# Moving rows between partitions in batch 1 of an attention kernel: DMA transfers in place of VectorE copies

## The chip, the cores and the metric

The kernel runs on one core of a Trainium2 chip. The metric is the device time of one execution in microseconds (us). TensorE is called PE here, VectorE DVE, ScalarE ACT, GpSimd POOL, and SyncE SP; SP computes nothing in this kernel, it issues the DMA transfers.

## What is computed

Three layers run one after the other: an attention over hash buckets, a mixing layer (a Fourier transform over both axes, a normalisation, a feed-forward network) and a gated convolution. Only the first is touched by the change:

```python
def _attn_ref(q, k, v, proj):                 # q, k, v: 2 batches x 8 heads x 768 rows x 64
    scale = 1.0 / np.sqrt(D)
    q_bits = (np.einsum('bhsd,dk->bhsk', q, proj) > 0).astype(np.int64)   # proj: 64 x 6
    k_bits = (np.einsum('bhsd,dk->bhsk', k, proj) > 0).astype(np.int64)
    powers = 2 ** np.arange(n_bits)
    q_bucket = np.sum(q_bits * powers, axis=-1)
    k_bucket = np.sum(k_bits * powers, axis=-1)
    mask = q_bucket[:, :, :, None] == k_bucket[:, :, None, :]
    scores = scale * np.matmul(q, k.transpose(0, 1, 3, 2))
    scores = np.where(mask, scores, -1000000000.0)
    ...                                       # softmax over the last axis
    return np.matmul(attn, v).astype(np.float32)
```

The attention's output x (2 x 768 x 512) goes through `_moe_ref` (u = x + real part of the transform of x, then u + relu(norm(u) W1) W2) and `_moe2_ref` (sigmoid of a causal convolution, times x W, times W').

## The kernel before

The heads of a batch are taken two at a time: four pairs g = 0 to 3 in each of batches 0 and 1. For a pair, `prep(g)` makes the operands of the score matmuls, and then three units of 256 query rows follow (`pair` and `unit_out`), each with two heads and two blocks of 128 rows.

`prep` splits q and k into a high and a low fp16 part (`st`), transposes both with one DMA transpose each (line 248) into the tile `tb` (128 partitions: high and low part, each 64 deep), and fills a second tile `ta`, whose rows are contracted in a second matmul of the same scores. Three of `ta`'s pieces are rows of `tb` or `ta` that must stand on other partitions, and the function `move` brings them there:

- line 251, q: `ta[0:64, 0]` from `tb[64:128, 0]`, 64 partitions x 1536 fp16 values
- line 252, k: `ta[0:64, 1]` from `tb[0:64, 1]`, the same size
- line 266, the sign features of the hash: `ta[64:96, 1]` from `ta[96:128, 0]`, 32 partitions x 1536 values. DVE writes these signs at line 265 from the products `bt` of line 260 (PE).

A score matmul (line 326) reads `ta` and then `tb`. DVE reads the scores out of PSUM into `e` with their maximum (line 338), ACT takes the exponential (line 343) and its fp16 part (line 112), POOL the rest (line 120), and a DMA transpose (line 355, `at<-a`) turns the result, so that PE can multiply it with v (line 364, `pv`).

`QJ` is a pair of strings, one for each batch; each letter says who performs one of the three moves: `v` is DVE, `s` a DMA issued by SP.

A scheduler that simulates the program places the instructions: what stands in the code in one order is merged, for each engine, into one fixed list. So batch 1's pair 0 is prepared while batch 0's last units run, the mixing layer of batch 0 (lines 480 to 682) is woven into batch 1's pair 0, and the feed-forward network of batch 0 (lines 712 and 729) into batch 1's pairs 1 to 3. Each engine takes its list in order: an instruction that waits holds up all that stand behind it. This holds for SP too. Its list contains the loads of q, k and v (lines 211 and 213), the loads of weights into a ring of two slots (line 433, `ring`), which DVE unpacks with three instructions (lines 419 to 421), and all DMA transposes. A DMA that reads what another DMA wrote is issued once SP has seen the first one land.

Of the kernel before, what the change touches and what calls it, by code (L numbers as in the profile page):

```python
# [46 lines left out]
LEFT = 512  # L47
WB = 512
QW = {None: "s", "w2": "s"}
QJ = ('vvv', 'vvv')  # L50
TPE = {(0, g, i, 1): 'a' for g in range(4) for i in (1,)}
PPE = {(0, 1): 'a'}
HI = {}
# [24 lines left out]
def attention_fft_mix_gated_kernel(  # L78
# [121 lines left out]
    def attention(b, P, after=None):  # L200
# [15 lines left out]
        def move(o, i, eng):  # L216
            if eng in "vga":
                copy_of(o, i, 1.0, eng)
            else:
                nc.sync.dma_start(out=o, in_=i)  # L220
# [9 lines left out]
        def prep(g):  # L230
# [12 lines left out]
            for y in range(2):  # L243
# [3 lines left out]
                else:  # L247
                    marks[b, "prep", g] = nc.sync.dma_start_transpose(
                        out=tb[:, y].rearrange("p h (c t) -> p (h c) t", t=128), in_=it
                    ).ins  # L250
            move(ta[0:64, 0], tb[64:128, 0], QJ[b][0])
            move(ta[0:64, 1], tb[0:64, 1], QJ[b][1])
            for n in range(2):
# [9 lines left out]
                for hh in range(2):  # L263
                    o = slice(64 * hh, 64 * hh + 64)
                    nc.vector.tensor_scalar(ta[64:128, 0, hh, r], bt[o, :], lim[o, 0:1], lim[o, 1:2], ALU.is_gt, ALU.mult)
            move(ta[64:96, 1], ta[96:128, 0], QJ[b][2])
            values(g, lv)
            tq[g] = ta, tb

        def values(g, lv):  # L270
            vt = P.vt.tile([128, 2, C, 2, D], FP16, tag="vt", name="vt")
            v2 = vt.rearrange("p h c x d -> p (h c) x d")
            with after_mark([marks["first", PF]] if not b and g == 0 else []):
                split(v2[:, :, 0, :], v2[:, :, 1, :], lv, VS, 'av' if not b and g < 1 else VH[b])
            va[g] = vt
# [828 lines left out]
```

## Time and profile before

| what | us |
|---|---|
| median of three runs | 684.14 |
| lowest and highest of them | 683.41 and 687.34 |
| the profiled execution's own time | 682.82 |
| its span, first to last instruction | 681.0 |
| PE busy in the span | 578.8 (85%) |
| DVE busy | 521.9 (77%) |
| ACT busy | 367.0 (54%) |
| POOL busy | 283.4 (42%) |

The profile is that of one execution; the span leaves out 1.8 us that lie around it. Where times of instructions are given they count from the start of the span. Busy times of the whole span hide that the stages have different limits, so the stretch from 132 to 381 us, where batch 1's attention runs, has to be read by itself.

### The profile page before, as it was taken

What the parts mean: (1) busy time and instruction counts of PE and PEld (TensorE: products, weight loads), DVE (VectorE), ACT (ScalarE), POOL (GpSimd) and SP (SyncE); (2) the same over time, 40 slices, a digit from 0 to 9 for tenths busy, and PEclk for the clock granted to TensorE, in tenths of its full rate; (3) what the DMA queues carried; (4) which work ended last, traced back from release to release, by engine and by line L of the source; (5) the groups of instructions that cost most, each with busy time, mean ns of one, the idle gap of its engine ahead of it and who ended that gap; (6) DMA issues with size and microseconds to landing.
All of it is one profiled execution on the core that took longest, in us unless ns stands there. A gap on an engine that the chain in (4) does not pass through costs nothing.

```text
span 681.0 us, 13258 instructions
## 1 busy us (share of the span) xinstructions
PE 578.8 (85%) x5078; PEld 443.7 (65%) x5078; DVE 521.9 (77%) x1007; ACT 367.0 (54%) x752; POOL 283.4 (42%) x312
## 2 busy tenths in 40 slices
PE   6787767866537789986999999988999999999997
PEld 3454535544324657665677788877677788888864
DVE  6978797799999898998865369996999256282682
ACT  4997979996764337875888426311334202111242
POOL 3868668875864415767656301260232100000000
PEclk8787779787866689999999999998799999999999
DMA  8989999989776354689785764000000000000001
GB/s 300 236 139 234 210 234 217 225 133 179 149 153 139 110 124 109 148 155 198 139 145 102 135 183 151 6 1 1 1 32 32 32 1 2 2 1 1 1 32 63
DMA packets 177888, 75.84 MB, mean 111 GB/s; under 512 B 162464, under 2 KB 168224, under 8 KB 177824
## 3 DMA queue, kind: packets, MB, share of 16 engines
q1 hardware_dynamic: 177248, 74.88, 50.6%
q8 instruction: 40, 0.66, 0.4%
q14 instruction: 24, 0.20, 0.1%
q10 hardware_dynamic: 576, 0.10, 0.1%
HBM read 32.50 MB, written 3.15 MB: 52 GB/s over the span
## 4 chain that ended last, share of the span: by engine, by line
PE 30%; DVE 13%; ACT 3%; issue 3%; POOL 1%; ACTq 0%; DVEq 0%; POOLq 0%
PE f L729 14%; PE f L712 8%; DVE gt L754 3%; PE op L873 2%; PE vp L848 1%; PE vp L770 1%; ACT a L112 1%; PE op L795 1%; DVE x L126 1%; DVE gt L117 1%; DVE h L694 1%; ACT e L343 1%; DVE cen L644 1%; PE mp L601 1%; DVE gt L821 1%
## 5 line engine op out<-in xcount | busy, mean ns | idle before, releaser
L120 POOL TENSOR_TENSOR a<-e,a 128x384 f16<-128x384 f32 x184 | 174.9, 976 | 93.0 <-ACT a L112 75.7
L712 PE MATMUL f<-un,w 128*128 128x256 f16 x1152 | 135.3, 274 | 3.2 <-DVE h L694 2.7
L729 PE MATMUL f<-h,w 128*128 128x256 f16 x1152 | 133.1, 274 | 0.9 <-DVE h L694 0.9
L712 PEld LDWEIGHTS <-w 128*128 128x128 f16 x1152 | 112.7, 98 | 22.0 <-issue 4.8
L729 PEld LDWEIGHTS <-w 128*128 128x128 f16 x1152 | 112.2, 98 | 17.8 <-issue 3.2
L338 DVE TENSOR_SCALAR_CACHE_REDUCE e<-sc 128x768 f32<-128x768 f32 x96 | 90.5, 949 | 16.1 <-POOL a L120 12.6
L364 PE MATMUL pv<-at,vt 128*64 128x256 f16 x864 | 75.3, 323 | 26.4 <-DMA at<-a 23.4
L343 ACT ACTIVATE e<-e,mx 128x768 f32<-128x768 f32 x96 | 89.1, 929 | 3.7
L364 PEld LDWEIGHTS <-vt 128*64 128x64 f16 x864 | 58.0, 130 | 44.7 <-issue 23.7
L112 ACT ACTIVATE a<-e 128x768 f16<-128x768 f32 x96 | 80.1, 839 | 1.0
L326 PE MATMUL sc<-ta 96*128 96x384 f16 x192 | 51.4, 352 | 29.8 <-DVE e L338 26.0
L694 DVE SCALAR_TENSOR_TENSOR h<-f,h 128x512 f16<-128x512 f32 x48 | 32.7, 686 | 32.7 <-ACT h L693 32.6
L326 PE MATMUL sc<-tb 128*128 128x384 f16 x192 | 51.9, 353 | 0.0
L693 ACT ACTIVATE h<-f 128x512 f16<-128x512 f32 x48 | 28.4, 591 | 43.1 <-PE f L712 42.9
L326 PEld LDWEIGHTS <-ta 96*128 96x128 f16 x192 | 17.0, 100 | 51.1 <-issue 44.6
L700 DVE SCALAR_TENSOR_TENSOR xb<-f,xb 128x256 f32<-128x256 f32 x24 | 13.7, 615 | 43.6 <-PE f L729 43.6
L120 POOL TENSOR_TENSOR w<-wt,w 128x256 f16<-128x256 f32 x40 | 30.1, 764 | 35.4 <-ACT w L112 35.2
L112 ACT ACTIVATE x<-xb 128x256 f16<-128x256 f32 x24 | 11.7, 535 | 54.0 <-DVE xb L700 53.5
L420 DVE SCALAR_TENSOR_TENSOR wt<-ring,wt 128x256 int32<-128x256 int32 (+1 forms) x60 | 37.0, 623 | 0.6
L821 DVE SCALAR_TENSOR_TENSOR gt<-xb,cw,gt 128x256 f32<-128x256 f32 x60 | 37.2, 680 | 0.0
L112 ACT ACTIVATE wt<-wt 128x256 f32<-128x256 f32 x40 | 16.2, 412 | 37.7 <-DVE wt L421 36.7
L421 DVE SCALAR_TENSOR_TENSOR wt<-ring,wt 128x256 int32<-128x256 int32 (+1 forms) x60 | 35.7, 602 | 0.5
(147 smaller groups left out, 930.6 us busy)
## 6 DMA issues: line engine op xcount, KB each, us to landing
ring<-in_moe_w_ch_dram SPq DMA_DIRECT2D x40, 256.0 KB, 3.1
ring<-in_moe_w_ch_dram SPq DMA_DIRECT2D x12, 512.0 KB, 5.0
lv<-in_v_dram SPq DMA_DIRECT2D x8, 384.0 KB, 4.5
out_dram<-ob SPq DMA_DIRECT2D x12, 256.0 KB, 2.0
lq<-in_q_dram SPq DMA_DIRECT2D x7, 384.0 KB, 3.9
lk<-in_k_dram SPq DMA_DIRECT2D x7, 384.0 KB, 4.6
ring<-in_moe_w_val_dram SPq DMA_DIRECT2D x4, 512.0 KB, 5.6
ring<-in_moe_w_out_dram SPq DMA_DIRECT2D x4, 512.0 KB, 3.9
```

The costliest lines, as they stand in the source:

```text
L112: return nc.scalar.activation(out=o, in_=i, func=ACTF.Copy, scale=s)
L120: return (nc.gpsimd if eng == "g" else nc.vector).tensor_tensor(out=o, in0=i0, in1=i1, op=op)
L326: nc.tensor.matmul(out=s[:, n, 0:384], lhsT=z[0:rows, 0, hh, r], rhs=z[0:rows, 1, hh, n * 384:n * 384 + 384], start=(x == 0), stop=(x == 1),)
L338: nc.vector.tensor_scalar(e.rearrange("p (a b) -> p a b", a=2), s, -(PEN * PEN) / 2, None, ALU.max, ALU.max, accum_out=m[:, 0:1]).ins
L343: marks["first", 2 + j] = nc.scalar.activation(out=e, in_=e, func=ACTF.Exp, bias=m[:, 1:2], scale=SC, accum_out=sums[:, hh, j:j + 1]).ins
L364: nc.tensor.matmul(out=p[64 * hh:64 * hh + 64, :], lhsT=va[g][:, hh, c, x, :], rhs=at[hh][:, :, y, c, :], start=(c == 0 and n == 0), stop= ...
L420: nc.vector.scalar_tensor_tensor(out=tmp, in0=hi, scalar=-0x40000000, in1=tmp, op0=ALU.bitwise_and, op1=ALU.bitwise_or)
L421: return nc.vector.scalar_tensor_tensor(out=dst, in0=lo, scalar=29, in1=tmp, op0=ALU.logical_shift_right, op1=ALU.bitwise_or)
L694: nc.vector.scalar_tensor_tensor(out=h[:, 1, f:f + 2, :], in0=p, scalar=0.0, in1=h[:, 0, f:f + 2, :], op0=ALU.max, op1=ALU.subtract)
L712: nc.tensor.matmul(out=p[:, o, :], lhsT=w1[:, i, kd, (f + o) * 128:(f + o) * 128 + 128], rhs=un[:, j, kd, :], start=(k == 0), stop=(k == 3 ...
L729: nc.tensor.matmul(out=p[:, o, :], lhsT=w2[:, i, f, (d + o) * 128:(d + o) * 128 + 128], rhs=h[:, j, f, :], start=(k == 0), stop=(k == 3 * ...
L821: nc.vector.scalar_tensor_tensor(out=o, in0=src, scalar=cw[:, d, j:j + 1].bitcast(FP32), in1=o, op0=ALU.mult, op1=ALU.add)
```

## The change

The second string of `QJ` becomes `sss`: in batch 1, all three moves of each of the four pairs are DMA transfers from SBUF to SBUF, issued by SP (line 220), where DVE copies (line 116) stood. Batch 0 keeps its copies.

```diff
--- before
+++ after
@@ -47,7 +47,7 @@
 LEFT = 512
 WB = 512
 QW = {None: "s", "w2": "s"}
-QJ = ('vvv', 'vvv')
+QJ = ('vvv', 'sss')
 TPE = {(0, g, i, 1): 'a' for g in range(4) for i in (1,)}
 PPE = {(0, 1): 'a'}
 HI = {}
```

Since the scheduler places every instruction, the lists of all engines differ from this point on. On SP, where batch 1's pair 0 is prepared (the transposes `tb<-st` are those of this pair, `at<-a` those of batch 0's last units):

```order
 L213 DMA lv<-in_v_dram 128x2x384
 L248 DMA_TRANSPOSE tb<-st 128x12x128 x2
+L220 DMA ta<-tb 64x1536
+L213 DMA lq<-in_q_dram 128x2x384
+L220 DMA ta<-tb 64x1536
+L213 DMA lk<-in_k_dram 128x2x384
+L355 DMA_TRANSPOSE at<-a 128x12x128 x3
+L220 DMA ta<-ta 32x1536
+L355 DMA_TRANSPOSE at<-a 128x12x128 x3
```

The two moves of q and k now stand between the transposes that they wait for and the `at<-a` transposes; the move of the signs stands among these.

On DVE, the same place (`e,mx<-sc` reads scores, `xb<-pv` scales a unit's output, `ta<-bt` makes the signs, `wt<-ring` unpacks weights):

```order
 L126 SCALAR_TENSOR_TENSOR vt<-lv,vt 128x12x64
-L116 COPY ta<-tb 64x1536
-L338 TENSOR_SCALAR e,mx<-sc 128x768
-L116 COPY ta<-tb 64x1536
-L338 TENSOR_SCALAR e,mx<-sc 128x768
+L338 TENSOR_SCALAR e,mx<-sc 128x768 x2
 L380 TENSOR_TENSOR xb_67<-pv,xb_67 128x256
 L265 TENSOR_SCALAR ta<-bt,lim 64x384 x2
 L371 RECIPROCAL r_1915<-r_1915 128x4
```

The two copies are gone and the rest closes up. Behind this piece the third copy is gone as well, and the mixing layer's instructions (lines 480 to 483, 126, 117) come earlier relative to the first scores of batch 1: on PE, twelve matmuls of line 503 now stand ahead of these scores.

On SP, at the last pair of batch 1, pair 3:

```order
 L248 DMA_TRANSPOSE tb<-st 128x12x128
-L355 DMA_TRANSPOSE at<-a 128x12x128 x24
+L433 DMA ring_2128<-in_moe_w_ch_dram 128x512
+L220 DMA ta<-tb 64x1536 x2
+L355 DMA_TRANSPOSE at<-a 128x12x128 x4
+L220 DMA ta<-ta 32x1536
+L355 DMA_TRANSPOSE at<-a 128x12x128 x20
```

Here too the moves of q and k stand ahead of all transposes that are left, and the signs' move behind four of them.

## Rows read from the trace of the kernel before

**Rows 1.** The page: busy time by engine, and the second feed-forward matmul's group.

```profile
PE 578.8 (85%) x5078; PEld 443.7 (65%) x5078; DVE 521.9 (77%) x1007; ACT 367.0 (54%) x752; POOL 283.4 (42%) x312
...
L729 PE MATMUL f<-h,w 128*128 128x256 f16 x1152 | 133.1, 274 | 0.9 <-DVE h L694 0.9
```

**Rows 2.** Busy time by stretch: bounds and length, then engines, PE clock, DMA share.

```profile
132.00:145.00 13.00, 9.05 (x103) 6.53 (x103) 12.71 (x23) 12.51 (x28) 7.76 (x8) 0.87 0.85 158
...
187.00:204.00 17.00, 5.92 (x49) 3.86 (x47) 16.94 (x31) 10.27 (x22) 11.46 (x12) 0.60 0.81 158
...
222.00:243.00 21.00, 14.47 (x122) 12.67 (x121) 18.44 (x41) 7.85 (x17) 7.53 (x10) 0.67 0.41 113
243.00:256.00 13.00, 12.49 (x87) 8.80 (x86) 11.20 (x25) 4.11 (x11) 1.97 (x3) 0.87 0.41 108
...
289.00:307.00 18.00, 15.29 (x160) 11.62 (x159) 17.63 (x35) 13.94 (x32) 12.28 (x15) 1.00 0.88 162
307.00:323.00 16.00, 11.14 (x106) 8.32 (x106) 13.27 (x24) 9.62 (x23) 11.55 (x13) 1.00 0.89 195
...
340.00:381.00 41.00, 40.66 (x390) 31.74 (x388) 22.48 (x45) 33.56 (x74) 22.32 (x26) 1.00 0.76 139
```

**Rows 3.** Groups of the copies, both batches: busy us, mean ns, idle before them.

```profile
L116 DVE COPY ta<-tb 64x1536 f16<-64x1536 f16 x14 | 9.8, 697 | 5.8 <-DMA tb<-st 5.6
L116 DVE COPY ta<-ta 32x1536 f16<-32x1536 f16 x7 | 5.2, 742 | 0.2
```

**Rows 4.** Timeline of DVE: start us, us, instruction, [idle before it].

```profile
132.54 0.55 DVE L116 COPY ta<-tb 64x1536 f16<-64x1536 f16 x1
...
133.99 0.85 DVE L116 COPY ta<-tb 64x1536 f16<-64x1536 f16 x1
...
144.82 0.56 DVE L116 COPY ta<-ta 32x1536 f16<-32x1536 f16 x1
...
146.86 0.96 DVE L338 TENSOR_SCALAR_CACHE_REDUCE e<-sc 128x768 f32<-128x768 f32 x1
...
147.75 1.22 DVE L126 SCALAR_TENSOR_TENSOR y<-yf,y 128x1024 f16<-128x1024 f32 x1
...
195.56 1.55 DVE L116 COPY ta<-tb 64x1536 f16<-64x1536 f16 x2
...
306.67 1.16 DVE L116 COPY ta<-ta 32x1536 f16<-32x1536 f16 x1
...
```

**Rows 5.** Timeline of SP: start us, us that issuing took, transfer.

```profile
127.45 4.47 SPq L248 DMA_TRANSPOSE tb<-st  x2
...
133.17 2.09 SPq L355 DMA_TRANSPOSE at<-a  x1
...
135.35 4.03 SPq L355 DMA_TRANSPOSE at<-a  x1
...
319.75 2.37 SPq L248 DMA_TRANSPOSE tb<-st  x1
...
322.23 1.46 SPq L355 DMA_TRANSPOSE at<-a  x1
```

**Rows 6.** DMA issues: transfer, count, KB each, median us from issue to landing.

```profile
out_dram<-ob SPq DMA_DIRECT2D x12, 256.0 KB, 2.0
...
at<-a SPq DMA_TRANSPOSE x88, 4.2
lq<-in_q_dram SPq DMA_DIRECT2D x2, 192.0 KB, 3.3
...
tb<-st SPq DMA_TRANSPOSE x12, 4.6
```

**Rows 7.** Timeline of PE, same columns as DVE's.

```profile
141.40 3.47 PE L364 MATMUL pv<-at,vt 128*64 128x256 f16 x36 [3.04 <-DMA at<-a]
...
145.43 0.48 PE L326 MATMUL sc<-ta 96*128 96x384 f16 x2
...
242.60 0.61 PE L712 MATMUL f<-un,w 128*128 128x256 f16 x4
...
307.88 0.48 PE L326 MATMUL sc<-ta 96*128 96x384 f16 x2 [1.17 <-DVE ta L116]
```

## The prediction

> **What bounds the kernel now.** I read the busy times of the whole span first [rows 1]: PE is busy for 85% of it and DVE for 77%, which looks like a kernel that PE alone limits. The table by stretch then says where that is true [rows 2]. From 340 us PE works for 40.66 of 41.00 us: there only PE's own work counts. Between 132 and 243 us it is DVE: 12.71 of 13.00 us, 16.94 of 17.00, 18.44 of 21.00, while PE is busy for about two thirds and its granted clock stands at 0.60 to 0.87, a mean between its two levels (1.2 and 2.4 GHz, 0.5 and 1.0). What DVE does there (batch 0's last units, batch 1's pair 0, the mixing layer) ends in the first feed-forward matmul at 242.60 [rows 7], and from then on PE has work for almost every gap. So a microsecond of DVE taken out before 242.60 is worth a microsecond, if nothing else becomes late; a microsecond taken out later is worth at most what PE idles: 0.51 us between 243 and 256, 2.71 between 289 and 307, 4.86 between 307 and 323 [rows 2]. The third thing to see is the DMA share: 0.85, 0.81, 0.88, 0.89 in the stretches where pairs are prepared [rows 2]. The twelve new transfers meet a loaded DMA.
>
> **What the change removes.** Twelve copies. The group means, 697 and 742 ns [rows 3], would price them at 4 x (2 x 0.70 + 0.74) = 8.6 us, but the place decides. Pair 0 has its three at 132.54, 133.99 and 144.82: 0.55 + 0.85 + 0.56 = 1.96 us. Pair 1 has its first two at 195.56: 1.55 us [rows 4]. These five, 3.5 us, lie in the stretch that DVE bounds. The other seven lie behind 242.60. Pair 1's third and pair 2's first two stand between 243 and 256 us; PE idles there for 0.51 us, so they are worth 0 to 0.5; I take 0.4. Pair 2's third, 1.16 us at 306.67, has PE waiting for it (1.17 us ahead of 307.88 [rows 7]) and is treated below. Pair 3's lie where PE has other work. In the new order three unpacking instructions and one of the mixing's (line 609) also slip behind the first feed-forward normalisation; they must be done in any case, and I count them at nothing.
>
> **What one transfer costs.** The trace has no SBUF-to-SBUF move. Moves of q and k are 64 x 1536 x 2 bytes = 192 KB, those of the signs 96 KB. The nearest rows [rows 6] are a store of 256 KB, 2.0 us from issue to landing, as the lower end; a load of exactly 192 KB, 3.3 us; and the transposes of a loaded queue, 4.2 and 4.6 us, as the upper end. I take 3.3, the same size. The copy took 0.55 to 1.16 us, so the data arrives some 2 to 3 us later than before, and in exchange nobody computes.
>
> The Trainium skill, SBUF — State Buffer, section "Door 1: The DMA port swizzle", speaks against such transfers: 64 partitions reach only 8 of 16 ports, as 32 do, and run at about 218 GB/s. With the fixed 2 us that the next section of that page gives, an estimate is 2.9 us for 192 KB; with all ports it would be 2.5 us. No row here shows such a transfer; by 2.9 in place of 3.3 the sum below would be 0.4 us better.
>
> **What the waits cost.** The two first moves of a pair can be issued only when the transposes `tb<-st` have landed, and while SP waits for that, the transposes `at<-a` stand behind.
>
> Pair 0: SP was done issuing both `tb` transposes at 131.92 and started the first `at<-a` at 133.17 [rows 5]. The second copy began at 133.99, so both halves of `tb` had landed by then [rows 4]. Now SP issues the second move at about 134.0, then a load of k, and reaches `at<-a` at about 134.9: 1.7 us later. It matters because PE waits 3.04 us for just these transposes, till 141.40 [rows 7]; the next one took 4.03 us to issue [rows 5], so the queue was full. PE's `pv` moves from 141.40 to 143.1. In the new order twelve matmuls of line 503 follow, about 3.47 x 12/36 = 1.2 us, ahead of batch 1's first scores, which stood at 145.43: 145.43 + 1.7 + 1.2 = 148.3. DVE stood at this place at 146.86; without the copies, and with the instruction of 1.22 us (`y<-yf`) that now comes ahead, it is there at 146.86 - 1.96 + 1.22 = 146.1, and needs the line 503 results. So it idles for 2.2 us. Bounds: with no delay of `at<-a` 0.5, and with the two moves taking DMA time from it as well (1.3 us more, the 3.3 of the load less the 2.0 of the store) 3.5.
>
> Pair 1: SP waits similarly, but DVE's next use of these transposes' units lies far behind: 0. The signs' move comes after line 265 and has more than ten microseconds of feed-forward matmuls ahead of the scores in PE's list: 0. While SP waits for `tb` of pair 2, the weight loads behind it could not go earlier, since their ring slot is released by DVE only then: 0; without this cover it would be the rest of a landing, up to 3 us.
>
> Pair 2: the signs' move stands on SP behind a transpose and a weight load, so it starts at 306.67, where the copy started, at best, and lands 3.3 us later, at 310.0, where the copy ended at 307.83 [rows 4]; I add 0.4 for what stands ahead of it. PE, which was ready for these scores at 307.88 - 1.17 = 306.71 [rows 7], has 11 more feed-forward matmuls ahead of them in the new order, 11 x 133.1/1152 = 1.3 us [rows 1], and is ready at 308.0. Its stall becomes 2.4 us instead of 1.2: 1.2 more. Bounds: -1.2 (hidden, the old stall vanishes) and +3.5 (a landing of 4.6 us, and another 1.4 on the queue).
>
> Pair 3: the second `tb` transpose was issued at 319.75, and `at<-a` followed at 322.23 [rows 5]. Now SP holds until 319.75 + 4.6 = 324.4 and two moves: 2 to 3 us later. Afterwards SP used to wait for POOL's results, so it catches up, and PE has feed-forward matmuls: 0, bounds 0 and +3.
>
> **The sum.** -3.5 (five copies) + 2.2 (DVE idle at pair 0) - 0.4 (243 to 256) + 1.2 (pair 2) + 0 = -0.5 us. On the profiled execution's 682.8 this is 682.3; the median of the runs is 684.1, so I forecast 683.6. All of it lies before 340 us; behind that the lists of PE and DVE do the same work in nearly the same order.
>
> **Rivals.**
> - *The waits are hidden.* The queue has room, `at<-a` does not come later at pair 0 (0.5), pair 2's stall vanishes (-1.2), and 0.5 between 243 and 256: -3.5 + 0.5 - 0.5 - 1.2 = -4.7, 679.4 us. For it: DVE at 98% and 99.6% [rows 2] is the clearest number of the table. Against: PE did wait 3.04 us for the transposes that are now held up.
> - *SP becomes the bound (slower).* The moves wait on SP for a landing, and behind them stand the transposes that PE's `pv` waits for. With the upper bounds at pairs 0, 2 and 3: -3.5 + 3.5 + 3.5 + 3 = +6.5, 690.6 us. It decides from the point at which the waits cost more than 3.9 us together, and gets beyond 0.5% from 7.3 us. For it: DMA shares of 0.85 to 0.89 just where the moves go. Against: PE and DVE have work that doesn't depend on these transposes.
> - *DVE's copies were not what held the stretch.* If the mixing's chain (DVE, PE and ACT in turn) sets 242.60, the five copies are worth little, as the 2.56 us of DVE idle between 222 and 243 would suggest, and the waits mostly fall into gaps as well: -1 to +2, 683 to 686. The same verdict as my forecast.
>
> The Trainium skill, SBUF — State Buffer, also states, in "Who interferes with whom", that copies of DVE can hold a port that POOL shares, one of them blocked for the whole instruction. The trace agrees in kind: the 32-partition copy took 0.56 us at one place and 1.16 at another [rows 4]. POOL is not what bounds here, so the sum leaves it out.
>
> **How the numbers follow.** About 0.5% (3.4 us) is what a measurement of this kernel can tell from no change. My forecast with the third rival, 44%; faster 26%, where the bounds of the first rival reach; slower 30%, since three places have an upper bound of 3 us or more and the scheduler's new lists were made with its own idea of a transfer's time. The forecast's own range is 681.2 (pair 2 hidden, 2.4 less) to 687.2 (pairs 0 and 2 at their upper bounds, 1.3 and 2.3 more). Range for 8 in 10: 679.0 (the first rival) to 689.0 (most of the second).
>
> **What would show it.** Right: the twelve copies gone, DVE idle of about 2 us at 145 to 149 us with a release by PE line 503 or a DMA; `at<-a` at pair 0 starting near 135; the first matmul of line 712 1 to 2 us earlier than 242.60. The moves should land in 2.0 to 4.6 us. Wrong would be: line 712 earlier by 3.5 us and still early at 340 (first rival), or PE waiting for `at<-a` or `ta` for several us at pairs 2 and 3 (second).

## The result, and the profile after

The changed kernel takes 690.63 us, median of its runs (688.56 to 693.58); the kernel before took 683.77 beside it. The ratio is 1.0094, 95% interval 1.0074 to 1.0114: slower by 0.9%, some 6.5 us. The forecast was 683.6 with a range up to 689.0. The profiled execution took 691.06 us, with a span of 689.3.

The page of the changed kernel, and of the group table the weight unpacking's first instruction (line, engine, operation, count | busy us, mean ns | idle before it and what ended it); the last line is the same group in the kernel before:

```profile
PE 580.0 (84%) x5078; PEld 443.3 (64%) x5078; DVE 520.6 (76%) x995; ACT 367.7 (53%) x752; POOL 281.4 (41%) x312
...
L419 DVE TENSOR_SCALAR wt<-ring 128x256 int32<-128x256 int32 (+1 forms) x60 | 34.1, 573 | 9.3 <-DMA ring<-in_moe_w_ch_dram 8.8
...
L419 DVE TENSOR_SCALAR wt<-ring 128x256 int32<-128x256 int32 (+1 forms) x60 | 30.4, 512 | 2.4 <-DMA ring<-in_moe_w_ch_dram 2.2
```

The twelve copies are gone (995 instructions on DVE against 1007 [rows 1]), but DVE's busy time fell by 1.3 us only, and DVE now stands idle for 9.3 us in front of line 419, nearly all of it waiting for weights; before it was 2.4. Busy time by stretch, as in [rows 2]:

```profile
243.00:256.00 13.00, 10.95 (x87) 8.46 (x86) 8.53 (x19) 3.73 (x9) 1.34 (x2) 0.91 0.60 134
289.00:307.00 18.00, 12.72 (x126) 9.26 (x125) 17.74 (x32) 12.40 (x29) 12.27 (x13) 0.94 0.65 138
307.00:323.00 16.00, 13.78 (x113) 10.81 (x112) 12.58 (x22) 9.09 (x22) 9.64 (x12) 0.96 0.88 164
323.00:340.00 17.00, 11.56 (x104) 6.39 (x103) 14.44 (x28) 12.06 (x28) 10.53 (x13) 0.87 1.02 223
```

The kernel before in the last of these stretches, which [rows 2] leaves out:

```profile
323.00:340.00 17.00, 15.93 (x159) 11.28 (x157) 14.02 (x28) 13.26 (x30) 11.10 (x13) 1.00 0.74 141
```

Between 243 and 256 us DVE lost 2.67 us of work and PE 1.54 against [rows 2]. Between 289 and 307 PE lost 2.57, and had 2.64 more in the next stretch. The largest loss is at pair 3: between 323 and 340 PE worked for 4.37 us less than before. A second profiled execution of the changed kernel (e15 below) shows which of these places come back:

```profile
243.00:256.00 13.00, 13.00 (x99) 9.25 (x92) 9.43 (x20) 4.09 (x10) 1.40 (x3) 0.90 0.65 151
...
323.00:340.00 17.00, 11.41 (x104) 6.13 (x102) 14.60 (x28) 12.20 (x28) 10.36 (x13) 0.90 1.04 224
```

There PE is busy for the whole of the first stretch, and the loss of the last one is as large. The granted clock from 289 to 323, 1.00 in [rows 2], is 0.94 and 0.96 in the first execution, a mean with some time at the lower of the two levels, and PE had waited there. The timeline of DVE has the places (start us, us, instruction, [idle before it]):

```profile
148.64 1.10 DVE L117 TENSOR_SCALAR z<-zp 128x512 f32<-128x512 f32 x1 [2.33 <-PE zp L503]
...
251.40 0.29 DVE L419 TENSOR_SCALAR wt<-ring 128x256 int32<-128x256 int32 x1 [3.21 <-DMA ring<-in_moe_w_ch_dram]
251.73 1.37 DVE L265 TENSOR_SCALAR ta<-bt,lim 64x384 f16<-64x384 f32 x2
...
324.33 0.29 DVE L419 TENSOR_SCALAR wt<-ring 128x256 int32<-128x256 int32 x1 [4.58 <-DMA ring<-in_moe_w_ch_dram]
```

The first idle place is the one forecast at pair 0. The other two were not. SP's timeline shows what stood in front of the weights (start us, us that issuing took; L220 is a move):

```profile
240.70 3.56 SPq L248 DMA_TRANSPOSE tb<-st  x2
...
244.95 2.10 SPq L220 DMA_DIRECT2D ta<-tb  x2
247.15 1.02 SPq L433 DMA_DIRECT2D ring<-in_moe_w_ch_dram  x2
...
253.13 0.57 SPq L220 DMA_DIRECT2D ta<-ta  x1
...
254.84 7.43 SPq L433 DMA_DIRECT2D ring<-in_moe_w_ch_dram  x4
...
310.81 0.55 SPq L220 DMA_DIRECT2D ta<-ta  x1
...
314.52 4.43 SPq L355 DMA_TRANSPOSE at<-a  x2
...
331.07 7.20 SPq L355 DMA_TRANSPOSE at<-a  x4
```

At 244.95 SP issues q's and k's moves of pair 2, then two weight loads, and from 248.17 to 253.13 nothing: the next in its list is the move of pair 1's signs, whose source VectorE finishes at 253.1 (line 265, at 251.73). Four weight loads stand behind it. The load that VectorE waits for until 251.40 is not among them: it was issued by 248.17, behind q's and k's moves, and VectorE unpacks from 259.06 on, after the four had begun to go out at 254.84, without a wait for weights until 324.33. Ahead of the wait that ends at 324.33, SP issues three `at<-a` transposes with one weight load between them (from 314.52 to 321.48); no move stands in that piece. PE's timeline:

```profile
242.14 2.12 PE L712 MATMUL f<-un,w 128*128 128x256 f16 x15
...
253.25 3.81 PE L640 MATMUL mean<-xb,mean_w 128*128 128x256 f32 x8 [2.05 <-DVE ta L265]
...
304.43 0.72 PE L260 MATMUL bt<-tb,pj 128*32 128x384 f16 x12 [3.32 <-DVE ta L265]
...
307.99 5.78 PE L729 MATMUL f<-h,w 128*128 128x256 f16 x50
313.91 0.48 PE L326 MATMUL sc<-ta 96*128 96x384 f16 x2
...
325.58 2.15 PE L364 MATMUL pv<-at,vt 128*64 128x256 f16 x35 [1.86 <-DMA at<-a]
...
334.74 0.48 PE L326 MATMUL sc<-ta 96*128 96x384 f16 x2 [2.15 <-DVE e L338]
```

Three things are to be seen. PE waits 2.05 us at 253.25 for VectorE, which had waited for weights. The 3.32 us at 304.43 are another case: between 289 and 307 VectorE works for 17.74 of 18 us, and its new list puts line 265 later. And pair 2's scores, at 307.88 before [rows 7], stand at 313.91: their signs' move was issued at 310.81, and PE's list has 50 feed-forward matmuls in that place, where the kernel before has 39:

```profile
302.28 4.43 PE L729 MATMUL f<-h,w 128*128 128x256 f16 x39
```

Counted from the start, 304 feed-forward matmuls (lines 712 and 729) run ahead of these scores in the trace of the changed kernel, and 267 in that of the kernel before. PE does not idle in front of the scores, but batch 1's attention is 6 us late. At pair 3 PE does idle, for transposes and for scores (the last two lines).

### The profile page after: what moved, and what is told of

Read it like the earlier page. It is cut to its first block, busy times and chain, and to the rows that moved or that the text cites. A ratio compares the mean times of both kernels' runs of the same rounds, so it can differ in the third digit from the quotient of the medians.

```text
span 689.3 us, 13266 instructions
## 1 busy us (share of the span) xinstructions
PE 580.0 (84%) x5078; PEld 443.3 (64%) x5078; DVE 520.6 (76%) x995; ACT 367.7 (53%) x752; POOL 281.4 (41%) x312
## 4 chain that ended last, share of the span: by engine, by line
PE 39%; DVE 35%; DMA 8%; issue 8%; ACT 5%; POOL 5%; SPq 0%; ACTq 0%; DVEq 0%; POOLq 0%
PE f L729 12%; PE f L712 10%; PE pv L364 6%; POOL a L120 4%; DVE gt L754 4%; DMA at<-a 4%; DVE e L338 3%; DVE wt L419 3%; DVE wt L420 3%; PE sc L326 3%; DVE wt L421 3%; DVE z L120 2%; PE op L873 2%; DMA ring<-in_moe_w_ch_dram 2%; ACT e L343 2%
## 5 line engine op out<-in xcount | busy, mean ns | idle before, releaser
L120 POOL TENSOR_TENSOR a<-e,a 128x384 f16<-128x384 f32 x184 | 171.7, 957 | 92.8 <-ACT a L112 71.1
L729 PE MATMUL f<-h,w 128*128 128x256 f16 x1152 | 136.1, 277 | 0.3 <-POOL w L120 0.2
L419 DVE TENSOR_SCALAR wt<-ring 128x256 int32<-128x256 int32 (+1 forms) x60 | 34.1, 573 | 9.3 <-DMA ring<-in_moe_w_ch_dram 8.8
L421 DVE SCALAR_TENSOR_TENSOR wt<-ring,wt 128x256 int32<-128x256 int32 (+1 forms) x60 | 39.1, 653 | 0.6
L420 DVE SCALAR_TENSOR_TENSOR wt<-ring,wt 128x256 int32<-128x256 int32 (+1 forms) x60 | 37.4, 627 | 0.6
```

The lines of the kernel that those rows point to most:

```text
L120: return (nc.gpsimd if eng == "g" else nc.vector).tensor_tensor(out=o, in0=i0, in1=i1, op=op)
L419: nc.vector.tensor_scalar(tmp, hi, 3, 0x3FFFFFF8, ALU.logical_shift_left, ALU.bitwise_and)
L420: nc.vector.scalar_tensor_tensor(out=tmp, in0=hi, scalar=-0x40000000, in1=tmp, op0=ALU.bitwise_and, op1=ALU.bitwise_or)
L421: return nc.vector.scalar_tensor_tensor(out=dst, in0=lo, scalar=29, in1=tmp, op0=ALU.logical_shift_right, op1=ALU.bitwise_or)
L729: nc.tensor.matmul(out=p[:, o, :], lhsT=w2[:, i, f, (d + o) * 128:(d + o) * 128 + 128], rhs=h[:, j, f, :], start=(k == 0), stop=(k == 3 * ...
```

## Experiments

Between them the theories were: QUEUE (SP takes its list in order; a move waits there, and weight loads and transposes wait behind it), LANDING (a transfer's landing takes the place of a copy at every pair), and ORDER (the edit gives every engine a new list, and that costs or gains by itself).

### One part of the change alone

```
-QJ = ('vvv', 'vvv')
+QJ = ('vvv', 'ssv')
```

> Batch 1: only q's and k's rows go by DMA, the signs stay VectorE copies. QUEUE (the moves of q and k wait on SP for the transposed tile tb to land, and weight loads and at<-a transposes stand behind them in SP's in-order list): most of the +6.8 us, so 4 to 7 us over the kernel before. LANDING (a landing of 2.9 us takes the place of a copy in front of PE at every pair and every move): two thirds of it at most, 3 to 5 us. ORDER (any edit of the lists gives another order, with gains and losses that do not add): e1 and e2 together differ from 6.8 by more than 3 us.

686.37 us, ratio 1.0035 (1.0010 to 1.0060): +2.4 us.

```
-QJ = ('vvv', 'vvv')
+QJ = ('vvv', 'vvs')
```

> Batch 1: only the signs' rows go by DMA, q and k stay VectorE copies. QUEUE: 0 to 2 us over the kernel before, since the signs' move waits on SP for VectorE's comparison alone and few weight loads stand behind it. LANDING: 2 to 3 us, since scores wait for the signs at four pairs, 0.8 copy against 2.9 landing. ORDER: as in e1, no sum with it to 6.8.

694.12 us, ratio 1.0145 (1.0117 to 1.0174): +9.9 us. The signs alone cost more than all twelve moves together, the opposite of what QUEUE expected of the two kinds, and e1 and e2 make 12.3, not 6.8: ORDER, as far as sums go.

For e3 and e4 the choice is made by pair:

```
-QJ = ('vvv', 'vvv')
+QJ = ('vvv',) * 4, ('sss', 'sss', 'vvv', 'vvv')
...
-            move(ta[0:64, 0], tb[64:128, 0], QJ[b][0])
+            move(ta[0:64, 0], tb[64:128, 0], QJ[b][g][0])
```

> Batch 1: only pairs 0 and 1, prepared before the feed-forward part starts, move by DMA. QUEUE: -1.5 to 0.5 us against the kernel before, as after's first feed-forward matmul came 0.5 us earlier with these two pairs moved. LANDING: about half of the loss, +3 us. ORDER: -1.5 to 0.5 too, if the loss lies in the reordered stretch behind 243 us; but also anything, since the stretch behind it is ordered anew.

685.32 us, ratio 1.0018 (0.9994 to 1.0041): +1.2 us, no difference that these runs can tell.

```
+QJ = ('vvv',) * 4, ('vvv', 'vvv', 'sss', 'sss')
```

> Batch 1: only pairs 2 and 3, prepared beside the feed-forward part, move by DMA. QUEUE: +5.5 to +8 us, the whole loss, with VectorE again idle for weight loads (3.2 us near 250 and 4.6 us near 323 in the changed kernel). LANDING: about +3 us. ORDER: e3 and e4 together differ from 6.8 by more than 3 us.

692.28 us, ratio 1.0117 (1.0087 to 1.0147): +8.0 us. e3 and e4 make 9.2, less than 3 us from 6.8, so ORDER does not show in this sum. The loss goes with the pairs prepared beside the feed-forward part, where SP also brings the weights. LANDING, which would share it out evenly, falls.

### The order held

All four kernels above have lists of their own. To change the moves and nothing else, the next ones write every engine's list out and hold it: a table has the instructions of each engine in the wanted order, and each is tied behind the one ahead of it, which sets an order and is not meant to add a wait. No run holds an order and changes nothing else, so what holding costs by itself is not measured; the nearest runs, e6 and e16, are 0.9 us above and 0.2 below the kernel before.

```
+ORDER = ...
+def pin(tc, nc):
...
+        for x, y in zip(row, row[1:]):
+            tc.add_manual_dep(ins[y], ins[x].name, _m.DependencyInfo(_m.DependencyClass.NoSync, _m.DependencyReason.DATA), reason="pin")
...
         attention_fft_mix_gated_kernel(tc, *args)
+        pin(tc, nc)
```

e5, SP's list at pair 2, with QJ of batch 1 `'sss'` and all other lists as in the kernel before:

```
 tb<-st
 ring
 tb<-st
+ta<-tb x2 (pair 2)
 ring
+ta<-ta (pair 1)
 ring
 ring
```

> The twelve copies of batch 1 are DMAs, but every other instruction of every engine keeps the place that it has in the kernel before (its order is written out and held); the moves stand on SP behind the same SP instruction as in the changed kernel, and behind both transposes of their pair. MOVES (the DMAs cost the time: SP held up, weight loads late, landings): +5 to +8 us over the kernel before. ORDER (the new order of the lists costs it, not the DMAs): -3 to +1 us.

691.11 us, ratio 1.0095 (1.0058 to 1.0133): +6.5 us.

e6, the same place:

```
 tb<-st
 ring
 tb<-st
+ta<-tb (pair 2, q)
 ring
+ta<-tb (pair 2, k)
 ring
 ring
+ta<-ta (pair 1)
```

> As e5, the kernel before's order held on every engine, but each move stands on SP where SP was at the time at which VectorE began the copy in the trace of the kernel before, so later than in e5 and seldom with SP waiting. MOVES: less than e5, 0 to +5 us; if SP's waiting is the cost, 3 us or more below e5. ORDER: -3 to +1 us, as e5.

685.05 us, ratio 1.0013 (0.9991 to 1.0034): +0.9 us. The lists of e5 and e6 are the same on every engine but for the places of nine of the twelve moves on SP (the other three stand alike); the difference is 6 us (691.11 against 685.05). SP's and DVE's timelines of e5 at pair 2:

```profile
244.44 2.97 SPq L220 DMA_DIRECT2D ta<-tb  x2
247.50 0.53 SPq L433 DMA_DIRECT2D ring<-in_moe_w_ch_dram  x1
254.99 0.56 SPq L220 DMA_DIRECT2D ta<-ta  x1
```

```profile
250.54 0.29 DVE L419 TENSOR_SCALAR wt<-ring 128x256 int32<-128x256 int32 x1 [3.34 <-DMA ring<-in_moe_w_ch_dram]
...
259.24 0.29 DVE L419 TENSOR_SCALAR wt<-ring 128x256 int32<-128x256 int32 x1 [4.28 <-DMA ring<-in_moe_w_ch_dram]
```

and of e6:

```profile
245.27 0.54 SPq L433 DMA_DIRECT2D ring<-in_moe_w_ch_dram  x1
247.21 0.47 SPq L220 DMA_DIRECT2D ta<-tb  x1
250.14 1.40 SPq L433 DMA_DIRECT2D ring<-in_moe_w_ch_dram  x2
253.27 0.56 SPq L220 DMA_DIRECT2D ta<-ta  x1
```

```profile
248.82 0.30 DVE L419 TENSOR_SCALAR wt<-ring 128x256 int32<-128x256 int32 x1 [1.71 <-DMA ring<-in_moe_w_ch_dram]
```

Between 244.4 and 255 us one weight load gets out in e5, three in e6, and VectorE waits 7.62 us for weights at the two places shown (3.34 + 4.28) against 1.71. So in the old order QUEUE is shown, with its place and its price.

```
-all engines: order of the kernel before
+all engines: order of the changed kernel
 QJ = ('vvv', 'vvv')
```

> The reverse: VectorE makes all copies as in the kernel before, but every other instruction of every engine stands in the changed kernel's order; each copy stands on VectorE where VectorE was when the changed kernel issued the move. MOVES: within 2 us of the kernel before, since nothing is held up by a move on SP. ORDER: +5 to +9 us, the changed kernel's loss without its DMAs.

693.48 us, ratio 1.0130 (1.0096 to 1.0164): +8.9 us, without one DMA move, as ORDER expected. Every engine's list is that of the changed kernel, SP's without the moves. So the changed kernel's order is slow by itself, with the copies put back into it. PE waits for line 265 there too, a weight load is late, now behind transposes only, and SP gets to pair 3's `at<-a` as late as in the changed kernel (331.07), with no move in front:

```profile
306.20 1.15 PE L260 MATMUL bt<-tb,pj 128*32 128x384 f16 x12 [3.58 <-DVE ta L265]
```

```profile
327.01 0.29 DVE L419 TENSOR_SCALAR wt<-ring 128x256 int32<-128x256 int32 x1 [4.90 <-DMA ring<-in_moe_w_ch_dram]
```

```profile
331.43 21.58 SPq L355 DMA_TRANSPOSE at<-a  x7
```

The two waits answer to the changed kernel's 3.32 at 304.43 and 4.58 at 324.33; its first one, 3.21 at 251.40, is 0.68 us long in e7. With this, order and moves stand apart: in the old order the DMAs, placed late, cost 0.9 us; in the new order the copies cost 8.9 and the DMAs 6.5.

What the new order does is seen best by comparing the same instruction in each trace (found by its place in the program text, DVE's instructions; start before, then how much later it starts):

| instruction | before, us | changed | e7 (order, copies) | e6 (old order, moves late) |
|---|---|---|---|---|
| 36th weight unpacking (line 419) | 253.03 | +6.2 | +8.0 | +1.0 |
| 64th score step (line 338), pair 1 | 268.08 | +5.1 | +6.9 | +1.3 |
| 8th feed-forward step (line 694) | 297.08 | -11.0 | -9.3 | +1.3 |
| 48th weight unpacking | 305.79 | +9.8 | +12.2 | +1.3 |
| last score step, pair 3 | 381.71 | +7.2 | +10.0 | +1.3 |
| last feed-forward add (line 700) | 645.13 | +7.7 | +10.1 | +0.6 |

Feed-forward work of batch 0 went ahead by up to 11 us, batch 1's attention and the weights fell back by 5 to 10. From the last score step on, everything is late by what that step is late. The traces were apart before that: the first feed-forward matmul starts at 242.60, 242.1, 245.1 and 243.9, so up to 2.5 us of a column may be such drift.

### Which moves hold the queue

The changed kernel, its order held, one SP instruction moved:

```
 ta<-tb x2 (pair 2)
 ring
 ring
-ta<-ta (pair 1)
 ring
 ring
+ta<-ta (pair 1)
```

> The changed kernel, every engine's order held as it is, with one SP instruction moved: the move of pair 1's signs stands two weight loads later, behind the loads that it stood ahead of. QUEUE-SIGNS (that move waits on SP for VectorE's last comparison, SP issues nothing from 248.2 to 253.1 us, and VectorE waits 3.21 us for a weight load): 2.5 to 4.5 us faster than the changed kernel, so +2 to +4.5 us over the kernel before. ORDER-ONLY (the loss is the new order, whatever SP does): no change from the changed kernel, +6 to +7.5 us.

693.63 us, ratio 1.0133 (1.0093 to 1.0173): +9.1 us, above what either theory expected, with an interval that reaches into ORDER-ONLY's. The wait for weights at this place, 3.21 us in the changed kernel's first trace, is shorter here,

```profile
253.66 0.29 DVE L419 TENSOR_SCALAR wt<-ring 128x256 int32<-128x256 int32 x1 [1.70 <-DMA ring<-in_moe_w_ch_dram]
```

but the load it waits for stood ahead of the move already, and the wait is as short in the second trace of the changed kernel (e15), with the move in its old place:

```profile
251.15 0.29 DVE L419 TENSOR_SCALAR wt<-ring 128x256 int32<-128x256 int32 x1 [1.67 <-DMA ring<-in_moe_w_ch_dram]
```

The whole gained nothing, and the wait near 325 us is still there (4.87 us at 327.30). So QUEUE-SIGNS falls as the account of the changed kernel: with the other lists laid out as they are, the hold of this one move is not what sets the time.

In e6's list, one move earlier:

```
 ta<-tb (pair 2, k)
+ta<-ta (pair 1)
 ring
 ring
-ta<-ta (pair 1)
```

> As e6 (the kernel before's order, moves placed late), but pair 1's sign move alone in the early place that it has in e5, one weight load behind q's and k's moves of pair 2. QUEUE-SIGNS: +3 to +6 us over the kernel before, most of e5's 6.5. QUEUE-QK (q's and k's moves, which wait for tb to land, hold the loads): as e6, 0 to +2 us.

687.55 us, ratio 1.0056 (1.0031 to 1.0082): +3.8 us, 2.9 above e6. The one move placed early (at 253.34) holds SP from 247.4, and DVE waits for the load behind it:

```profile
246.94 0.47 SPq L220 DMA_DIRECT2D ta<-tb  x1
253.34 0.56 SPq L220 DMA_DIRECT2D ta<-ta  x1
253.95 13.44 SPq L433 DMA_DIRECT2D ring<-in_moe_w_ch_dram  x5
```

```profile
257.72 0.29 DVE L419 TENSOR_SCALAR wt<-ring 128x256 int32<-128x256 int32 x1 [4.41 <-DMA ring<-in_moe_w_ch_dram]
```

> As e6, but q's and k's moves of all four pairs in the early places of e5, signs late. QUEUE-SIGNS: 0 to +2.5 us over the kernel before. QUEUE-QK: +4 to +7 us, as e5.

687.82 us, ratio 1.0046 (1.0020 to 1.0072): +3.1 us, between what the two theories expected.

> As e6, but all four sign moves in the early places of e5, q and k late. QUEUE-SIGNS: +4 to +7 us over the kernel before, as e5. QUEUE-QK: 0 to +2 us, as e6.

688.44 us, ratio 1.0052 (1.0016 to 1.0087): +3.6 us, between them again. So in the old order q and k placed early cost 2.2 us over e6, the signs placed early 2.7, and both (e5) 5.6. The first two differences are no larger than the intervals that go into them; that both kinds hold the queue rests on the traces, where VectorE's waits for weights between 243 and 270 us make 2.1 us in e6, 4.0 in e10, 6.6 in e11 and 8.5 in e5. e11 differs from e9 by the move of pair 2's signs alone and is no slower, so of the signs it is pair 1's move that counts.

### SP's list or the others'

Both with QJ of batch 1 `'sss'`; first

```
-SP: e6's list
+SP: the changed kernel's list
 PE, DVE, ACT, POOL: the lists of the kernel before
```

> All copies of batch 1 are DMAs; PE, VectorE, ScalarE and GpSimd keep the order of the kernel before, and SP has the changed kernel's order whole: the early moves, and also the weight loads where the changed kernel has them among the transposes. QUEUE (SP's order is the cost, of whatever makes it): +5 to +9 us over the kernel before, as the changed kernel or a little over e5's 6.5. ENGINES (the new order of the four engines is the cost): +1 to +3 us, below e5.

711.77 us, ratio 1.0393 (1.0373 to 1.0413): +26.9 us.

and then

```
 SP: e6's list
-PE, DVE, ACT, POOL: the lists of the kernel before
+PE, DVE, ACT, POOL: the changed kernel's lists
```

> The reverse: all copies are DMAs, PE, VectorE, ScalarE and GpSimd have the changed kernel's order, and SP has e6's (the kernel before's, with late moves). QUEUE: -1 to +2.5 us against the kernel before, as e6. ENGINES: +6 to +9 us, as the changed kernel.

710.08 us, ratio 1.0361 (1.0334 to 1.0387): +24.7 us. Both miss every expectation. A list of SP and lists of the engines from different kernels do not seem to fit each other; in e12 VectorE stands idle for 31.3 us in front of line 419. So the loss of the changed kernel can't be handed to SP's list alone or to the other lists alone.

The changed kernel itself, without an edit, beside these two:

> The changed kernel once more beside e12 and e13: +6 to +8 us over the kernel before under every theory.

691.00 us, ratio 1.0090 (1.0067 to 1.0112): +6.2 us, as in the first comparison.

### What a copy is worth

```
             if eng in "vga":
                 copy_of(o, i, 1.0, eng)
+                if b:
+                    copy_of(o, i, 1.0, eng)
```

> The kernel before with its order held, and each of batch 1's twelve copies made twice on VectorE, one behind the other: what a copy's time on VectorE is worth. COPIES-COUNT (the sum of the prediction: five copies in front of the feed-forward part, 3.5 us, stand on the path; the seven behind it 0 to 1): +3.5 to +5 us. SLACK (VectorE waits elsewhere for what a copy would take, as e6's gain of nothing says): 0 to +2 us.

692.60 us, ratio 1.0108 (1.0081 to 1.0135): +7.4 us, above both expectations. The page, and the first feed-forward matmul (line 714 here; count: ns min/median/max, first and last start):

```profile
PE 584.1 (85%) x5078; PEld 445.9 (65%) x5078; DVE 528.6 (77%) x1019; ACT 367.4 (53%) x752; POOL 286.2 (41%) x312
```

```profile
L714 PE MATMUL f<-un,w x1152: 269/273/421, 247.1 to 632.5; 128*128 128x256 f16 x192
```

In this one trace the five extra copies ahead of the feed-forward part put its start off by 4.5 us (242.60 to 247.1), which leaves some 3 for the seven behind it. SLACK falls: VectorE is busy for 6.7 us more than before [rows 1], and the kernel is 7.4 us longer. That the time is not given back when the copies go (e6) then seems to lie with what the moves bring.

### Without the signs, and from another queue

e16 is e6 with `QJ = ('vvv', 'ssv')`; e17 is e16 with the moves issued by ScalarE:

```
-                nc.sync.dma_start(out=o, in_=i)
+                nc.scalar.dma_start(out=o, in_=i)
```

> As e6 (the kernel before's order held, moves late on SP), but the signs' copies of batch 1 stay on VectorE: only q's and k's eight copies are DMAs. If a copy's time counts on VectorE as e14 has it (about 1 us for 1 us), eight copies are 4.4 us and no scores wait for a sign move's landing: -4 to -1 us against the kernel before. If at<-a behind pair 0's moves on SP gives it back (VectorE idle 3.3 us at 148 us in e6): -1 to +1.5 us.

683.76 us, ratio 0.9997 (0.9977 to 1.0017): no difference, as the second reading has it. The trace agrees at pair 0: PE waits 4.12 us for `at<-a` (3.04 before [rows 7]), and VectorE, with two copies less to make, gets to its next score step at 147.88, not earlier than the 146.86 of before [rows 4].

> As e16, but q's and k's moves are issued by ScalarE, each where ScalarE was when VectorE began the copy in the kernel before, so that SP's list is untouched. If SP's held transposes and loads are what eats the gain: -4.5 to -1.5 us against the kernel before, and 1 us or more below e16. If the landing, or ScalarE's half us per issue, eats it: -1 to +2 us.

687.19 us, ratio 1.0051 (1.0033 to 1.0070): +3.5 us, a miss on the slow side. Most of the loss shows at pair 0: PE's wait there was 3.04 us at 141.40 before [rows 7], and is now

```profile
145.99 4.05 PE L364 MATMUL pv<-at,vt 128*64 128x256 f16 x36 [6.34 <-DMA at<-a]
```

and DVE, which was at its next score step at 146.86 [rows 4], is there at 151.60. Of the DMA issues of 125 to 150 us (KB each, median us to landing):

```profile
lk<-in_k_dram SPq DMA_DIRECT2D x1, 384.0 KB, 6.1
...
ta<-tb ACTq DMA_DIRECT2D x2, 192.0 KB, 7.5
```

The moves land beside the next pair's loads and take 7.5 us (5.0 in e16), the load of k takes 6.1 (4.6 before), and SP needs 6.79 us to issue the second of the `at<-a` transposes, where it needed 4.03 [rows 5]. That the moves delay these is the likely reading; no run moves them away from the loads alone.

> The changed kernel with all twelve moves issued by ScalarE instead of SP, every engine's order as it then comes out (nothing held). If SP's queue alone makes the loss: -3 to +2 us against the kernel before. If any order made around DMA moves puts work in front of batch 1's attention: +3 to +9 us.

This is the changed kernel with the same one-word edit (`nc.scalar`), in the order that it then gets. 682.69 us, ratio 0.9973 (0.9951 to 0.9996): 1.8 us faster than the kernel before, some 8 faster than the changed one. SP's timeline, and the first feed-forward matmul:

```profile
237.50 18.79 SPq L433 DMA_DIRECT2D ring<-in_moe_w_ch_dram  x8
```

```profile
L712 PE MATMUL f<-un,w x1152: 269/273/417, 238.6 to 622.2; 128*128 128x256 f16 x192
```

Eight weight loads go out in one row, with no move among them, and the feed-forward part starts 4.0 us earlier than at 242.60 [rows 7]. The wait at pair 0 is as long as in e17 (6.19 us), and yet the feed-forward part is not late in this order. So not every order made around DMA moves is slow; of those made with the moves on SP, e3's is not slow either, and e2's and e4's are slower than that of all twelve. e18 changes the queue and the order at once, so it doesn't tell which of the two gains. It beats both kernels, by 0.3% the one before: less than the 0.5% that the prediction called the limit of what can be told, with an interval that just leaves out 1.

## Why the prediction was wrong

**The bound, and what a copy is worth: right ahead of 242.60, too low behind it.** DVE bounds up to the first feed-forward matmul; five copies were priced at 3.5 us, and five more cost 4.5 in the one trace of e14. The seven behind were given 0.4 us and the place at pair 2; seven more cost some 3. One reading of [rows 2] was wrong: between 187 and 204 us PE is busy for 5.92 of 17.00 us, a third and not two thirds, which makes the case for DVE there stronger.

**Pair 0: right.** `at<-a` was forecast for about 134.9 and was issued at 134.44; DVE's idle time was forecast at 2.2 us and is 2.33, ended by line 503. A move was priced at 3.3 us; the median is

```profile
ta<-tb SPq DMA_DIRECT2D x8, 192.0 KB, 2.9
...
ta<-ta SPq DMA_DIRECT2D x4, 96.0 KB, 2.9
```

which is also the 2.9 us that was estimated from the Trainium skill (SBUF — State Buffer, "Door 1: The DMA port swizzle"). The agreement does not show that the ports are the reason: by the same working the 96 KB would be estimated at 2.5 us, and they took 2.9 too. Line 712 came 0.5 us earlier in one trace and 0.7 later in the other (e15), not 1 to 2 earlier.

**The order: the step that failed.** What the new lists move was priced as 1.3 us for "11 more feed-forward matmuls" ahead of pair 2's scores, and the unpacking that slips back was counted "at nothing". The 11 are right for the last piece (50 against 39), but over the whole way 37 more stand ahead of these scores (304 against 267). Batch 1's attention and the weights fell back by 5 to 10 us. e7 shows that this order is 8.9 us slow with the copies and without one DMA, while the DMAs in the old order cost 0.9 (e6). That the order came with the moves is plain from the edit; why the scheduler laid it out so is not shown.

**Pair 3: beyond its bound, and the same step.** 0 was taken, at most 3, since "PE has feed-forward matmuls". It had not: between 323 and 340 us PE worked for 4.37 us less than before. `at<-a` was issued at 331.07 instead of 322.23 [rows 5]. From the end of issuing the second `tb` transpose to `at<-a` SP took 3 us longer than before, as forecast, but that transpose was itself issued 6.5 us later (326.25), and in e7, without moves, `at<-a` comes at 331.43. The last comparison of the pair (line 265) is 4.5 us late.

**Pair 1 and the weights: wrong, but not what made the loss.** "While SP waits for `tb` of pair 2, the weight loads behind it could not go earlier, since their ring slot is released by DVE only then: 0." The next weight loads went out behind q's and k's moves at 247.15, and VectorE waited for weights there (3.21 us at 251.40 in one trace, 1.67 in the other), so an earlier load would have been of use. And of pair 1's signs only the landing was looked at, against PE's list; that the move itself stands on SP waiting for VectorE, with four weight loads behind it, was not seen. In the old order this hold has a price: 2.9 us for that one move (e9 against e6), 5.6 for all places (e5 against e6). In the changed kernel no wait of VectorE follows from the hold of the signs' move, and with the move put behind two of the loads (e8) nothing is gained; and without any move (e7) the loss is there all the same.

**Pair 2: mis-sized.** Its signs' move was to be issued at 306.67 and 0.4 us more; it was issued at 310.81, 3.6 us after VectorE had the signs (307.2), behind a transpose and a weight load. PE was to stall for 2.4 us and does not; the price is paid by attention, 6 us late at this place.

**The rivals.** "SP becomes the bound" gave 690.6 us, and 690.63 was measured. The agreement is luck. Its sum was made of waits behind moves at pairs 0, 2 and 3; moves do hold SP's queue (e5 against e6), but the changed kernel's loss is there without any move (e7).

**What stays open.** Which piece of the new order costs the time. The traces of the changed kernel, e7 and e8 all show the weight load late near 325 us, behind transposes, and the changed kernel's two show PE short of work at pair 3, but no run repairs that place alone. Early moves in the old order cost as much (6.5 us) by another way, and mixed lists cost 25 to 27, so the prices do not add.

## What to carry to other kernels

Where a scheduler makes the lists, price the new order as a change of its own, and hold the old order once, to learn whether the edit or the new order costs the time: here the twelve DMAs cost 0.9 us in the old order, and the new order 8.9 without them. When a copy becomes a DMA, price the place in the issuing queue before the transfer: a move waits in its queue for its source, and everything behind it waits as well, above all loads that the very engine needs that the move is waiting for. In the held order a later place in the same queue was worth 6 us. One word (`nc.scalar` for `nc.sync`) was worth 8 us, but with the order that came with it; in a held order the same word was 3.7 us slower (e17 against e16).

## What the runs showed of the hardware

**A copy's time is not all its own.** The groups of line 116 sum to 20.1 us before and 12.0 in the changed kernel, but DVE is busy for only 1.3 us less; the weight unpacking grew, line 419 from 30.4 to 34.1 us. Part of that goes with the new order. In e6, where the order is the old one, the same groups sum to 12.7, and DVE is busy for 517.1 us: 7.4 us of copies went and 4.8 us of busy time.

In the changed kernel's trace the 21 instructions of line 419 on 128 x 256 with POOL working for less than half of their time take 0.29 us on average, the 19 with POOL working beside them for most of it 0.77. The Trainium skill (SBUF — State Buffer, "Who interferes with whom") speaks of one engine blocked for the other's whole instruction; the two durations agree with that in kind. The prediction quoted this and left it out of the sum. DVE is busy for 517.1 us in e6 and 516.1 in e5, and only e5 is slow, so it is no cause of the loss by itself, but the busy time of a short copy overstates what removing it frees.

**One transfer, three prices.** The 192 KB move landed after 2.9 us in the median, after 5.4 at pair 0 in e6, and after 7.5 there in e17; both times two loads of 384 KB went out beside it. **Same program, other drift.** In two profiled executions of the changed kernel the first feed-forward matmul started at 242.1 and 243.3, and in e8, which has the same lists up to 248 us, at 245.0; a single trace settles nothing under 3 us here, unless the difference begins at the edit.
